# Opening of an adaLN transformer block: unread matmuls out, one term of a sum earlier, the first operand written in halves

## The chip, the cores and the metric

The kernel runs on one core of a Trainium2 chip. The metric is the device time of one execution in microseconds (us); where several executions are given, it is their median. The engines are named as in the profile: PE (TensorE: matmuls), PEld (its weight loads), DVE (VectorE), ACT (ScalarE), POOL (GpSimd), SP (SyncE, which issues most of the DMAs). Each engine runs its own instructions in order; they wait for each other by semaphores.

## The reference, cut to what matters

The reference is one transformer block with adaptive layer norm: a linear attention and a bilinear feed-forward part, on 2048 tokens of width 512. Six modulation vectors come out of one small product with a conditioning vector.

```python
mod = (_silu(c) @ w_mod).reshape(c.shape[0], 6, 1, -1)      # c: (1, 512), w_mod: (512, 3072)
sa, ca, ga, sb, cb, gb = (mod[:, 0], ..., mod[:, 5])
h = _layernorm(x, axis=-1) * (1 + ca) + sa
x = x + ga * _A_ref(h, A_wqkv, A_wo)      # linear attention, 32 heads
h = _layernorm(x, axis=-1) * (1 + cb) + sb
x = x + gb * _B_ref(h, B_w_gate, B_w_up, B_w_down)
```

Only the opening is touched: the layer norm of the first 512 tokens, the vectors `ca` (scale, vector 1) and `sa` (shift, vector 0), the modulated `h`, and the first product of `h` with the key weights.

## The kernel before, in words

Matmuls work in fp32r, and each fp32 product is made of three: a value is split into a high part `h` (rounded to fp32r) and a low part `l` (what is left), and high times high, high times low and low times high are summed in PSUM. The tokens are worked in four chunks of 512 (four groups of 128 tokens, called token groups 0 to 3), the width 512 in four blocks of 128. The order of all work is written out by hand: each engine executes its instructions in the order in which the program text issues them.

The opening does this for chunk 0:

- `keep_on(n)` issues n matmuls of 128x512 on a tile of zeros into a PSUM bank (`ps_idle`) whose result nobody reads (L155). There are 13 at the start, 5 after the small transpose of `c`, and then pairs between the steps of the opening.
- `n0.stats`, `rstd_of`, `nmr_of` and `xhat` are the layer norm: statistics on DVE, 1/std on POOL (L264), the negative mean times 1/std (`nmr`) on DVE (L269), the normalized tile on ACT (L279) or on DVE (L276, token group 3).
- `transpose_token(j)` turns token group j with four PE transposes (L293), one into each of four PSUM banks, so that bank k holds block k of the width for all 512 tokens.
- The columns of `ca` and `sa` for a block of 128 widths come from w_mod in two ways. `block_pe(v, b)` does the whole sum on PE: eight recorded matmuls with one column of output (L402). `half_sum(v, half, *ks)` adds four terms, one for each block of the conditioning vector, for 256 widths at a time: the first term on ACT (L178), the others on DVE (L182); `block_one(v, b)` then sums over the partitions with a matmul against ones (L413, two recorded instructions). `block_out(b)` copies the two columns of block b out of PSUM (L417, DVE).
- `mod_h(k)`, `mod_f(k)` and `mod_l(k)` make the modulated operand of block k: its high part on ACT (L424) from the PSUM bank, the unrounded value on ACT (L431), the low part on DVE (L436). `weight_h(k)` (ACT, L441) and `weight_l(k)` (DVE, L444) split the key weight of block k.
- `cells(*tk, parts)` is the product itself, one 128x512 matmul for token group t, block k and part (L453): part 0 is high times high, part 1 high times the weight's low part, part 2 low times high. The first ones use token groups 0 and 1, parts 0 and 1, then token groups 2 and 3, then part 2 of all four.

The loads are issued by SP and ACT at the start in the order of use; the change leaves them as they are.

Of the kernel before, what the change touches and what calls it, by code (L numbers as in the profile page):

```python
# [9 lines left out]
F32R = mybir.dt.float32r  # L10
AF = mybir.ActivationFunctionType
# [3 lines left out]
P = 128  # L15
# [7 lines left out]
def tile_adaln_block(  # L23
# [12 lines left out]
    nc = tc.nc  # L36
# [4 lines left out]
    NJ = 4  # L41
# [23 lines left out]
    def f32(ap):  # L65
        return ap.bitcast(F32)
# [3 lines left out]
    def T(p, tag, shape=(P, D), dt=F32, bufs=None):  # L70
        cnt[0] += 1
        return p.tile(list(shape), dt, tag="t" if p is tiles else tag, name=f"{tag}_{cnt[0]}", bufs=bufs)

    def B(tag, shape=(P, D), dt=F32):

        return T(tiles, tag, shape, dt)
# [76 lines left out]
    def keep_on(n):  # L153
        for _ in range(n):
            nc.tensor.matmul(ps_idle, idle[:, :P], idle, start=True, stop=True)  # L155
# [18 lines left out]
    def mod_acc(acc, raws, ks, on=None):  # L174
        for k in ks:
            if k == 0:
                if on:
                    on.activation(acc, raws[k], AF.Copy, scale=sc[:, 0:1])  # L178
                else:
                    nc.vector.tensor_scalar(acc, raws[k], sc[:, 0:1], None, op0=ALU.mult)  # L180
            else:
                nc.vector.scalar_tensor_tensor(acc, raws[k], sc[:, k:k + 1], acc, op0=ALU.mult, op1=ALU.add)  # L182
# [201 lines left out]
    n0 = norm[0]  # L384
    both = consts.tile([P, KD, 2], F32, name="both")
    ca, sa = both[:, :, 0], both[:, :, 1]
# [9 lines left out]
    def sums_in(b):  # L396
        return ps_idle if b == 1 else ps_m

    def block_pe(v, b):
        at, ps = at_of(v, b), sums_in(b)  # L400
        for k, raw in enumerate(half_of(v, b)):
            nc.tensor.matmul(ps[:, at:at + 1], raw, sc[:, k:k + 1], start=k == 0, stop=k == KD - 1)  # L402
# [3 lines left out]
    def half_sum(v, half, *ks, on=None):  # L406
        if 0 in ks:
            sums[v, half] = B("f")[:, :D // 2]
        mod_acc(sums[v, half], [raw_half[v, half][k // 2][:, k % 2] for k in range(KD)], ks, on)
# [6 lines left out]
    def block_out(b):  # L416
        nc.vector.tensor_tensor(both[:, b], sums_in(b)[:, 2 * b:2 * b + 2], unit, op=ALU.add)  # L417

    halves = {}

    def mod_h(k):
        halves[k] = (B("h", dt=F32R), B("h", dt=F32R), B("f"))
        h, l, f = halves[k]
        nc.scalar.activation(h, n0.ps[k], AF.Identity, scale=ca[:, k:k + 1], bias=sa[:, k:k + 1])  # L424

    def mod_f(k, on=None):
        h, l, f = halves[k]
        if on:
            on.tensor_scalar(f, n0.ps[k], ca[:, k:k + 1], sa[:, k:k + 1], op0=ALU.mult, op1=ALU.add)
        else:  # L430
            nc.scalar.activation(f, n0.ps[k], AF.Identity, scale=ca[:, k:k + 1], bias=sa[:, k:k + 1])  # L431
        n0.ps[k] = None
# [6 lines left out]
    def weight_h(k):  # L439
        wk.append((B("w", dt=F32R), B("w", dt=F32R)))  # L440
        nc.scalar.activation(wk[k][0], raw_k[k], AF.Copy)  # L441

    def weight_l(k, on=None):
        (on or nc.vector).tensor_tensor(wk[k][1], raw_k[k], f32(wk[k][0]), op=ALU.subtract)  # L444
# [3 lines left out]
    def cells(*tk, parts=(0, 1, 2)):  # L448
        for part in parts:
            for t, k in tk:  # L450
                h, l = halves[k][:2] if k in halves else n0.t[k]
                x, w = ((h, wk[k][0]), (h, wk[k][1]), (l, wk[k][0]))[part]
                nc.tensor.matmul(kps[t], x[:, t * P:(t + 1) * P], w, start=k == 0 and part == 0,  # L453
                                 stop=k == KD - 1 and part == 2)
# [13 lines left out]
    n0.rstd_of(2, 4)  # L468
    n0.transpose_token(0)
    half_sum(0, 0, 0, on=nc.scalar)  # L470
    n0.nmr_of(2, 4)
    n0.xhat(2)
    n0.xhat(3, on=nc.vector)
    keep_on(2)
    n0.transpose_token(1)
    block_pe(1, 0)
    half_sum(0, 0, 1, 2, 3)
    weight_h(0)
    keep_on(2)
    n0.transpose_token(3)  # L480
    n0.transpose_token(2)
    block_one(0, 0)
    block_out(0)
    weight_l(0)
    half_sum(1, 1, 0, on=nc.scalar)
    mod_h(0)
    keep_on(2)
    block_pe(1, 1)
    block_one(0, 1)
    mod_f(0)  # L490
# [10 lines left out]
    cells((2, 0), (3, 0), parts=(0, 1))  # L501
    cells(*four(0), parts=(2,))
    mod_h(1)
    weight_h(1)
    half_sum(0, 1, 1)
# [9 lines left out]
        block_one(1, b)  # L515
        block_one(0, b)
    cells(*four(1), parts=(1, 2))
    weight_l(2)
    block_out(2)
    block_out(3)  # L520
    mod_h(2)
    mod_f(2)
    mod_h(3)
# [1022 lines left out]
```

## Time and profile before

| what | value |
|---|---|
| three executions | 555.76 us median (555.52 to 556.16) |
| the profiled execution | 555.36 us |
| its span, first to last instruction | 553.5 us |
| mean granted TensorE clock | 0.998 |
| busy: PE, DVE, ACT, POOL | 547.2, 419.8, 297.1, 176.9 us |
| first cell (L453) | starts at 14.10 us |

Times of instructions are counted from the start of the span. A row of the timeline has the start, the length, the engine, the line and operation, output and inputs, their shapes, the number of instructions merged in the row, and in brackets the idle time of the engine before it and what ended it. Matmuls overlap: the next one starts before the one ahead has ended, so their cost is read from start to start.

### The profile page before, as it was taken

The numbers are of one execution on the slowest core, as the hardware profiler recorded it, in microseconds if no ns is written. First come the engines' busy times: TensorE is split into PE (matmuls) and PEld (weight loads), VectorE is DVE, ScalarE is ACT, GpSimd is POOL, SyncE is SP. The second block draws the span as 40 slices with busy tenths as digits, with TensorE's granted clock in tenths as the row PEclk, the third lists the DMA queues.
The fourth block names the chain that finished last, engine by engine and source line by source line (L and its number), as shares of the span: only waits on it lengthen the run. The fifth ranks groups of instructions, "written<-read, shape, count | busy, mean of one in ns | idle before, by whom it ended". The sixth has DMA issues, their size and how long they took to land.

```text
span 553.5 us, 8031 instructions
## 1 busy us (share of the span) xinstructions
PE 547.2 (99%) x2741; PEld 459.6 (83%) x2741; DVE 419.8 (76%) x755; ACT 297.1 (54%) x528; POOL 176.9 (32%) x183
## 2 busy tenths in 40 slices
PE   8999999999999999999999999999999999999997
PEld 6888888888888888888888888878888888888886
DVE  6868779978998998865655767854567877879696
ACT  4976858456567876653545355432442534453540
POOL 2000000003527645343556644400512524242400
PEclk9999999999999999999999999999999999999999
DMA  8900224203240045195888635499575534342004
GB/s 286 384 14 1 76 77 152 77 0 78 78 114 2 0 159 183 39 312 183 285 284 273 224 123 205 149 376 325 177 270 192 173 129 149 121 144 86 0 1 152
DMA packets 56752, 83.75 MB, mean 151 GB/s; under 512 B 6596, under 2 KB 21704, under 8 KB 56712
## 3 DMA queue, kind: packets, MB, share of 16 engines
q1 hardware_dynamic: 55872, 82.20, 43.4%
q10 hardware_dynamic: 840, 1.05, 0.5%
q8 instruction: 21, 0.34, 0.2%
q14 instruction: 19, 0.16, 0.1%
HBM read 53.54 MB, written 29.69 MB: 150 GB/s over the span
## 4 chain that ended last, share of the span: by engine, by line
PE 98%; DMA 1%; DVE 0%; ACT 0%; POOL 0%; issue 0%; DVEq 0%; POOLq 0%
PE bank L1037 38%; PE acc L1196 8%; PE acc L851 8%; PE bank L221 5%; PE bank L223 5%; PE bank L222 5%; PE acc L1120 4%; PE acc L1119 4%; PE acc L1121 4%; PE acc L372 3%; PE acc L370 3%; PE acc L371 3%; PE bank L286 2%; PE acc L453 2%; PE bank L826 1%; PE acc L776 1%
## 5 line engine op out<-in xcount | busy, mean ns | idle before, releaser
L1037 PE MATMUL bank<-h,w 128*128 128x512 f32 (+1 forms) x924 | 220.5, 391 | 0.0
L1037 PEld LDWEIGHTS bank<-h,w 128*128 128x128 f32 (+1 forms) x924 | 168.7, 186 | 36.6 <-issue 0.4
L1043 ACT ACTIVATE bank<-bank 128x512 f32<-128x512 f32 (+1 forms) x45 | 26.2, 581 | 131.2 <-PE bank L1037 130.9
L1000 POOL TENSOR_TENSOR w<-raw,w 128x256 fp32r<-128x256 f32 (+3 forms) x22 | 24.3, 1102 | 79.7 <-ACT w L993 64.9
L1220 DVE TENSOR_TENSOR x<-acc,x 128x256 f32<-128x256 f32 x108 | 39.2, 413 | 10.5 <-PE acc L1196 10.0
L1196 PE MATMUL acc<-w,kh 128*128 128x256 f32 x252 | 46.8, 282 | 0.0
L221 PE MATMUL bank<-w,h 128*128 128x512 f32 x112 | 44.1, 394 | 0.0
L1196 PEld LDWEIGHTS acc<-w,kh 128*128 128x128 f32 x252 | 41.4, 191 | 3.1 <-DVE x L1220 0.2
L223 PE MATMUL bank<-w,h 128*128 128x512 f32 x112 | 43.7, 390 | 0.0
L222 PE MATMUL bank<-w,h 128*128 128x512 f32 x112 | 43.7, 390 | 0.0
L851 PE MATMUL acc<-w,xh 128*128 128x512 f32 x128 | 40.7, 399 | 0.0
L1063 DVE TENSOR_TENSOR phi<-bank,g 128x512 f32<-128x512 f32 (+1 forms) x22 | 15.1, 687 | 29.9 <-PE bank L1037 28.4
L700 POOL TENSOR_TENSOR f<-h,zb 128x512 f32<-128x512 f32 x12 | 17.5, 1468 | 62.9 <-ACT zb L680 48.8
L264 POOL TENSOR_TENSOR rstd<-ve,half 128x4 f32<-128x4 f32 (+3 forms) x12 | 10.6, 881 | 82.5 <-DVE ve L261 70.1
L1093 DVE TENSOR_TENSOR g<-bank,u 128x512 f32<-128x512 f32 (+1 forms) x22 | 15.2, 689 | 28.3 <-ACT u L1043 26.9
L1119 PE MATMUL acc<-w,kh 128*128 128x512 f32 (+1 forms) x92 | 35.9, 390 | 0.0
L1120 PE MATMUL acc<-w,kh 128*128 128x512 f32 (+1 forms) x92 | 35.9, 390 | 0.0
L1121 PE MATMUL acc<-w,kl 128*128 128x512 f32 (+1 forms) x92 | 35.8, 389 | 0.0
L1196 PE MATMUL acc<-w,kl 128*128 128x256 f32 x126 | 35.6, 283 | 0.0
L1043 ACT ACTIVATE u<-bank 128x512 f32<-128x512 f32 (+1 forms) x44 | 26.2, 595 | 12.6 <-PE bank L1037 12.4
L1126 DVE TENSOR_TENSOR x<-acc,x 128x512 f32<-128x512 f32 x44 | 28.1, 681 | 6.0 <-PE acc L1121 6.0
L1000 POOL TENSOR_TENSOR w<-t,w 128x512 fp32r<-128x512 f32 (+1 forms) x22 | 29.7, 1348 | 0.0
(198 smaller groups left out, 1180.5 us busy)
## 6 DMA issues: line engine op xcount, KB each, us to landing
right<-w SPq DMA_DIRECT2D x56, 256.0 KB, 3.7
w<-right SPq DMA_DIRECT2D x56, 256.0 KB, 3.7
x<-in_A_x_dram SPq DMA_DIRECT2D x22, 256.0 KB, 5.3
raw<-in_w_mod_dram SPq DMA_DIRECT2D x22, 256.0 KB, 3.5
raw<-in_B_w_down_dram SPq DMA_DIRECT2D x20, 256.0 KB, 3.1
side_s<-h SPq DMA_DIRECT2D x16, 256.0 KB, 2.8
h<-side_s SPq DMA_DIRECT2D x16, 256.0 KB, 5.5
raw<-in_A_wqkv_dram SPq DMA_DIRECT2D x12, 256.0 KB, 5.4
```

The lines of the kernel that those rows point to most:

```text
L221: nc.tensor.matmul(ps, ah, bh, start=begin and i == 0, stop=False)
L222: nc.tensor.matmul(ps, ah, bl, start=False, stop=False)
L223: nc.tensor.matmul(ps, al, bh, start=False, stop=end and i == n - 1)
L851: nc.tensor.matmul(yps[i], x, y, start=fresh and k + n == 0, stop=k == KD - 1 and n == 2, skip_group_check=True)
L1000: sub = lambda out, x, y: (on or nc.gpsimd).tensor_tensor(out, x, f32(y), op=ALU.subtract)
L1037: mm = lambda x, y, **kw: nc.tensor.matmul(ps, x[:, k], y, skip_group_check=True, **kw)
L1043: nc.scalar.activation(out, x, AF.Copy)
L1119: nc.tensor.matmul(dn[j], hh[:n, a:b], dh[:n], start=i == 0, stop=False)
L1120: nc.tensor.matmul(dn[j], hh[:n, a:b], dl[:n], start=False, stop=False)
L1121: nc.tensor.matmul(dn[j], hl[:n, a:b], dh[:n], start=False, stop=i == n_of - 1)
L1196: mm = lambda x, y, **kw: nc.tensor.matmul(ps, x[:, a:b], y, skip_group_check=True, **kw)
L1220: nc.vector.tensor_tensor(xt[:, halves[at]], banks[b][:, part], xt[:, halves[at]], op=ALU.add)
```

## The change

Two of the pairs of unread matmuls go (the one ahead of the transposes of token groups 3 and 2, and the one ahead of `block_pe(1, 1)`); the pairs after token group 0 and the matmuls at the start stay. The second term of the first sum of the shift is issued on DVE ahead of `nmr_of(2, 4)` and no longer behind the normalization of token group 3. The first `mod_h` is written by two ACT instructions, for token groups 0 and 1 and for 2 and 3. `weight_l(2)` is issued behind the two `block_out` calls of blocks 2 and 3. The one-column sum `block_one(0, 0)` stands behind the transposes of all token groups, as before.

```diff
-    def mod_h(k):
-        halves[k] = (B("h", dt=F32R), B("h", dt=F32R), B("f"))
-        h, l, f = halves[k]
-        nc.scalar.activation(h, n0.ps[k], AF.Identity, scale=ca[:, k:k + 1], bias=sa[:, k:k + 1])
+    def mod_h(k, a=0, b=NJ):
+        if not a:
+            halves[k] = (B("h", dt=F32R), B("h", dt=F32R), B("f"))
+        h = halves[k][0][:, a * P:b * P]
+        nc.scalar.activation(h, n0.ps[k][:, a * P:b * P], AF.Identity, scale=ca[:, k:k + 1], bias=sa[:, k:k + 1])
...
     half_sum(0, 0, 0, on=nc.scalar)
+    half_sum(0, 0, 1)
     n0.nmr_of(2, 4)
     n0.xhat(2)
     n0.xhat(3, on=nc.vector)
     keep_on(2)
     n0.transpose_token(1)
     block_pe(1, 0)
-    half_sum(0, 0, 1, 2, 3)
+    half_sum(0, 0, 2, 3)
     weight_h(0)
-    keep_on(2)
     n0.transpose_token(3)
     n0.transpose_token(2)
     block_one(0, 0)
     block_out(0)
     weight_l(0)
     half_sum(1, 1, 0, on=nc.scalar)
-    mod_h(0)
-    keep_on(2)
+    mod_h(0, 0, 2)
+    mod_h(0, 2, 4)
     block_pe(1, 1)
...
     cells(*four(1), parts=(1, 2))
-    weight_l(2)
     block_out(2)
     block_out(3)
+    weight_l(2)
     mod_h(2)
```

Two pairs out are four matmuls; the halves add one ACT instruction. The other instructions are the same on each engine.

## The prediction

> **What bounds the kernel now.** I read the page first (busy shares and the chain of waits), then the windows view over the opening and the rest, then the waits, and last the timeline of the opening, row by row. The page:
>
> ```profile
> PE 547.2 (99%) x2741; PEld 459.6 (83%) x2741; DVE 419.8 (76%) x755; ACT 297.1 (54%) x528; POOL 176.9 (32%) x183
> PE 98%; DMA 1%; DVE 0%; ACT 0%; POOL 0%; issue 0%; DVEq 0%; POOLq 0%
> ```
>
> PE carries the span. The windows view, for all engines in the first row and for PE alone in the second (columns: stretch, its length, busy us and instructions of each engine, granted clock, DMA share, GB/s):
>
> ```profile
> 20.70:549.50 528.80, 528.73 (x2649) 444.61 (x2647) 405.18 (x715) 285.22 (x509) 173.59 (x166) 1.00 0.42 145
> 8.74:12.15 3.41, 3.41 (x28) 1.00 1.09 361
> ```
>
> From 20.70 us to the last matmul PE idles 0.07 us, so whatever the opening wins or loses at 20.70 arrives at the end. In the opening PE is full too, but partly with the unread matmuls. The timeline of the opening, PE first (start, length, engine, line, operation):
>
> ```profile
> 10.78 0.70 PE L155 MATMUL acc<-w 128*128 128x512 f32 x2
> 11.32 1.03 PE L293 MATMUL bank<-ident,n 128*128 128x128 f32 x8
> 12.31 0.35 PE L413 MATMUL acc<-ones,f 128*128 128x1 f32 x2
> 12.52 0.71 PE L155 MATMUL acc<-w 128*128 128x512 f32 x2
> 13.07 0.95 PE L402 MATMUL acc<-sc,raw 128*128 128x1 f32 x8
> 13.88 0.36 PE L413 MATMUL acc<-ones,f 128*128 128x1 f32 x2
> 14.10 1.40 PE L453 MATMUL acc<-w,h 128*128 128x512 f32 x5
> ```
>
> Matmuls overlap, so the cost of a group is the distance from its start to the next group's start: the two pairs (L155) cost 11.32 - 10.78 = 0.54 and 13.07 - 12.52 = 0.55, together 1.09 us. This is the most that removing them can give, beside small waits. Whether PE can use it depends on the chain through DVE and ACT:
>
> ```profile
> 9.12 0.49 ACT L178 ACTIVATE f<-raw,sc 128x256 f32<-128x256 f32 x1
> 9.98 0.16 DVE L269 SCALAR_TENSOR_TENSOR nmr<-mv,rstd 128x2 f32<-128x2 f32 x1 [0.81 <-POOL rstd L264]
> 10.18 0.81 ACT L279 ACTIVATE n<-x,nmr,rstd 128x512 f32<-128x512 f32 x1 [0.56 <-DVE nmr L269]
> 10.18 0.55 DVE L276 TENSOR_SCALAR n<-x,rstd,nmr 128x512 f32<-128x512 f32 x1
> 10.64 1.52 DVE L182 SCALAR_TENSOR_TENSOR f<-raw,sc,f 128x256 f32<-128x256 f32 x3
> 12.70 0.16 DVE L417 TENSOR_TENSOR both<-acc,unit 128x2 f32<-128x2 f32 x1 [0.54 <-PE acc L413]
> 12.78 0.69 DVE L444 TENSOR_TENSOR w<-raw,w 128x512 fp32r<-128x512 f32 x1
> 12.90 0.78 ACT L424 ACTIVATE h<-bank,both 128x512 fp32r<-128x512 f32 x1 [0.98 <-DVE both L417]
> 13.39 0.48 DVE L182 SCALAR_TENSOR_TENSOR f<-raw,sc,f 128x256 f32<-128x256 f32 x1
> 13.58 0.77 ACT L431 ACTIVATE f<-bank,both 128x512 f32<-128x512 f32 x1
> 14.24 0.51 ACT L178 ACTIVATE f<-raw,sc 128x256 f32<-128x256 f32 x1
> 14.36 1.00 DVE L182 SCALAR_TENSOR_TENSOR f<-raw,sc,f 128x256 f32<-128x256 f32 x2
> 14.64 0.78 ACT L424 ACTIVATE h<-bank,both 128x512 fp32r<-128x512 f32 x1
> ```
>
> **The change part by part.** All steps are built in the profiled execution's own time, 555.36 us (span 553.5, 1.9 around it); the median of the three runs is 555.76, 0.4 more, and the difference found is taken off that.
>
> *The second term ahead of nmr.* DVE sits idle for 0.81 us before nmr. ACT's first term ends at 9.61, so the second term can run from 9.65 (0.04 for the hand-over, as from nmr's end at 10.14 to 10.18) to 10.13. An independent DVE operation starts about 0.08 before the one ahead ends (10.64 against 10.73), so nmr starts at 10.05 instead of 9.98: nmr, the waiting ACT normalization and DVE's own lose 0.07. They now run from 10.25 to 11.06 and 10.80. The other two terms take 1.00 (the x2 row at 14.36), from 10.71 to 11.71; before, the sum ended at 12.16. Gain of the sum: 0.45.
>
> *First pair out.* PE is done with its eight L402 at 10.78, but the transposes of token 3 need DVE's normalization: 10.80 + 0.06, so 10.86. Eight transposes took at most 0.99 (11.32 to 12.31), so PE is through them by 11.85. The one-column sum L413 needs the sum plus the 0.15 that the hand-over took before (12.16 to 12.31): 11.86 instead of 12.31. So this pair gives 0.45, not 0.54, because the sum is next late. In the code that sum stands behind all transposes in both kernels; nothing moves there.
>
> *Second pair out.* L402 follows L413 after 0.21 (12.31 to 12.52), takes 0.81, and the second L413 0.22: the cells may start at 11.86 + 0.21 + 0.81 + 0.22 = 13.10 instead of 14.10. Their operand h must be there.
>
> *h in halves.* L417 moves from 12.70 to 12.25, and h from 12.90 to 12.45. No row shows a 128x256 activation out of PSUM. The ends are 0.39 (half of 0.78) and 0.78 (no saving); the nearest rows are the 128x256 ones at 0.49 and 0.51 on the same engine, and I take 0.52. The first half ends at 12.97, and the cells (0.05 later) could start at 13.02: hidden under PE's own 13.10, by a margin of 0.08. Undivided h would have ended at 13.23 and cost 0.18 here. But ACT pays: one activation hands over 0.10 before its end (12.90 to 13.58 for 0.78), so two halves hold it 0.84 and not 0.68. f starts at 12.45 + 0.84 = 13.29, against 13.58: ACT has gained 0.29 where DVE has 0.45. Queued behind it on ACT are the next sum's first term (14.24), h of the second block (14.64) and the second weight (15.30 below).
>
> From here the cells need, in turn, these rows:
>
> ```profile
> 15.28 0.68 DVE L436 TENSOR_TENSOR h<-f,h 128x512 fp32r<-128x512 f32 x1
> 16.02 0.53 PEld L453 LDWEIGHTS acc<-w,h 128*128 128x128 f32 x3 [0.26 <-DVE h L436]
> 15.30 0.63 ACT L441 ACTIVATE w<-raw 128x512 fp32r<-128x512 f32 x1
> 16.28 0.68 DVE L444 TENSOR_TENSOR w<-raw,w 128x512 fp32r<-128x512 f32 x1
> 16.88 1.00 DVE L182 SCALAR_TENSOR_TENSOR f<-raw,sc,f 128x256 f32<-128x256 f32 x2
> 17.95 0.95 PE L413 MATMUL acc<-ones,f 128*128 128x1 f32 x8
> 18.40 0.68 DVE L444 TENSOR_TENSOR w<-raw,w 128x512 fp32r<-128x512 f32 x1
> 19.00 0.22 DVE L417 TENSOR_TENSOR both<-acc,unit 128x2 f32<-128x2 f32 x2
> ```
>
> The low half of h (L436): DVE runs the weight's low part at 12.33, one term at 12.94, L417 of block 1 at 13.34 (its PE input is ready at 13.28), two terms from 13.42 to 14.42, and L436 at 14.34, the spacings as before; f is ready at 14.06. So 14.34 instead of 15.28, gain 0.94, and PE, which reaches that point at 13.10 + 1.92 = 15.02 (14.10 to 16.02 before), starts it at 15.09, 0.07 behind L436's end.
>
> The one-column sums at 17.95: the second of them needs the sum that ends at 17.88, which is queued behind L444 at 16.28, which needs ACT's weight at 15.30. ACT's side gains only 0.29: 15.01 to 15.64, L444 at 15.68, where DVE would be free at 14.34 + 1.00 = 15.34. So L444 gains 0.60, and the sum ends at 17.28. PE comes there at 17.95 - 0.94 = 17.01, spends 0.13 on the two instructions of the first sum and then waits until 17.28 + 0.15 = 17.43 where it had 18.08: **gain 0.65**. That is the new late link: 0.29 of the 0.94 goes into a wait for the ACT chain.
>
> *weight_l(2) behind L417.* Before, DVE held L417 until L444 let it go, at 19.00. PE's sums would end at 18.89 - 0.65 = 18.24 and L417 run at 18.28; with L444 ahead it would run at 17.80 + 0.60 = 18.40. The move gives 0.12 to ACT's next h. PE needs that h only at 20.70 - 0.65 = 20.05, while it ends at about 18.47 + 0.78 = 19.25, and the weight now ends at 19.1 and is needed at 20.5. Both are covered by the cells of block 1, so I count nothing.
>
> Sum: 0.65 us. With halves at 0.39, ACT would not bind and the gain is about 0.94; with halves at 0.78, it falls to about 0.1. My 0.52 gives 0.65, and I expect 0.5 to 0.8. **555.76 - 0.65 = 555.1 us.**
>
> **The rivals.** *The clock falls.* The unread pairs are also the only 512-column work between 9.5 us and the cells. What a cold TensorE costs, and what came before the one fall of the clock in this trace:
>
> ```profile
> 1.98 4.80 PE L155 MATMUL acc<-w 128*128 128x512 f32 x13 [1.98 <-DVE w L150]
> 20.70 2.92 PE L453 MATMUL acc<-w,h 128*128 128x512 f32 x12
> 548.04:551.46 3.42, 1.45 (x13) 1.00 0.67 224
> 551.46:553.47 2.01, 0.00 (x0) 0.00 (x0) 0.00 (x0) 0.00 (x0) 0.00 (x0) 0.50 0.14 47
> ```
>
> The first 13 matmuls took 4.80 us where 12 later took 2.92, 13 thus 3.15: one cold stretch costs 1.65. The clock fell to 0.50 after 3.42 us of which PE had worked 1.45. In the changed kernel PE stays occupied between 9.5 and 13.1 but for some 0.2 us, with transposes and one-column matmuls; before, 8.74 to 12.15 was full in the same loose sense and kept 1.00. Against the rival speaks that occupation; for it, that about 2.0 of those 3.6 us would be one-column matmuls, which move next to nothing. If it decides, one cold stretch over the cells gives 1.65 - 0.65 = 1.0 slower, 556.8; if the clock does not come back at the first chance, two give 2.65 slower, 558.4. It decides where such a stretch with under about 1.45 us of wide work counts as idle. The Trainium skill, "TensorE: Matmul & The Clock Gate", Part 1 (the HAM clock gate), says that the gate judges free-running windows of about 3.4 us, and Part 4 (PE-mode transpose) that a transpose doesn't count as busy in the same way. By that rule the pairs would be what kept the clock, and the time would be that of this rival in those runs whose window falls into the gap; the fall at the end of this trace agrees with a window of that length, and no row here shows a transpose stretch without pairs.
>
> *ACT's halves cost next to nothing and PE takes all.* The two pairs and the waits around them give 1.2 together: 554.5, faster than the bound. Against it speaks the ACT chain above.
>
> *Nothing arrives.* If halves cost as much as whole activations, 0.1 remains: 555.7. The same comes out if a load that doesn't move binds first. These rows say it doesn't:
>
> ```profile
> 9.13 1.85 SPq L111 DMA_DIRECT2D raw<-in_A_wqkv_dram  x3
> DMA to landing us min/median/max: 5.1/5.1/5.1
> 13.56 5.07 SPq L111 DMA_DIRECT2D raw<-in_A_wqkv_dram  x8
> ```
>
> The load behind L441's weight is issued at 9.13 and lands 5.1 later, at 14.2, for a use at 15.0. No issue moves past another in the queues.
>
> **How the numbers follow.** What a measurement of this kernel can tell from no change is about 0.2%, 1.1 us. My forecast has 0.64, nothing arrives 0.08, all taken 0.07, one cold stretch 0.09, more than one or another loss of that size 0.12. Faster by over 0.2% is the third alone, 0.07; slower the last, 0.12; the rest, 0.81, lies within. The forecast's own range is 554.8 to 555.5; the range given reaches from all taken to one cold stretch, 554.5 to 556.8.
>
> **What would show it.** Right: no L155 row after 9.7 us; cells (now L454) starting near 13.1; the second one-column sum near 17.4 with a PE wait of about 0.3 before it; 20.70 moved to about 20.05; halves of h near 0.52. Wrong: cells spaced 0.42 and not 0.23 apart, or a clock under 1.00 before 20 us (the first rival); halves above 0.6 with the second weight after 15.3 (nothing arrives); a new PE wait after 20 us.

## The result, and the profile after

The changed kernel takes 556.38 us (median of 22 executions, 555.52 to 559.48), the kernel before in the same sessions 555.98 (22, 555.27 to 556.66): a ratio of 1.0019, with a 95% interval of 1.0010 to 1.0028. The medians are 0.4 us apart; the ratio follows the means, 556.88 and 555.84, which are 1.0 apart. By either it is slower, where 0.65 us less was forecast. (One execution of a later experiment, e11, 682.98 us at a mean clock of 0.754, is of another, slow state and is left out.)

The executions of the changed kernel are not of one kind. Twelve have a mean granted clock of 0.998 or more; they take 555.52 to 556.41, and their middle, 555.94, is that of the kernel before. The other ten have 0.992 to 0.995 and take 556.90 to 559.48. The kernel before has none of the second kind in 108 executions. So two things are to be explained: why ten executions lose clock, and why the twelve that keep it gain nothing.

The profiled execution of the changed kernel is one that lost clock: 556.9 us, span 554.9. From its page, the busy shares and the granted clock in 40 slices:

```profile
PE 548.2 (99%) x2737; PEld 460.6 (83%) x2737; DVE 419.8 (76%) x755; ACT 297.2 (54%) x529; POOL 177.8 (32%) x183
PEclk9899999999999999999999999999999999999999
```

Four matmuls fewer, one activation more, as the diff says. The second slice, 13.9 to 27.7 us, shows an 8. The windows view (stretch, its length, busy us and instructions of PE, PEld, DVE, ACT and POOL, granted clock, DMA share, GB/s) around it:

```profile
10.20:13.62 3.42, 3.42 (x30) 3.22 (x30) 2.81 (x9) 2.69 (x6) 0.02 (x1) 1.00 1.09 359
13.62:17.03 3.41, 3.41 (x9) 2.66 (x9) 3.08 (x8) 3.41 (x8) 0.00 (x0) 0.50 1.06 388
17.03:20.44 3.41, 3.41 (x20) 2.94 (x20) 1.82 (x6) 1.65 (x4) 0.00 (x0) 1.00 1.05 386
```

The clock was halved for one stretch of 3.41 us. In the 3.42 us ahead of it PE is busy without a gap. The timeline of the changed kernel shows with what:

```profile
10.13 0.95 PE L402 MATMUL acc<-sc,raw 128*128 128x1 f32 x8
11.05 1.09 PE L293 MATMUL bank<-ident,n 128*128 128x128 f32 x8
12.07 0.35 PE L413 MATMUL acc<-ones,f 128*128 128x1 f32 x2
12.29 1.03 PE L402 MATMUL acc<-sc,raw 128*128 128x1 f32 x8
12.66 1.02 ACT L425 ACTIVATE h<-bank,both 128x256 fp32r<-128x256 f32 x2 [0.48 <-DVE both L417]
13.41 2.31 PE L454 MATMUL acc<-w,h 128*128 128x512 f32 x5
18.74 0.95 PE L413 MATMUL acc<-ones,f 128*128 128x1 f32 x8
26.95 0.39 PE L221 MATMUL bank<-w,h 128*128 128x512 f32 x1
```

One-column matmuls, transposes, and 0.21 us of the cells: no L155 row. The cells begin at 13.41, 0.69 earlier than before, but five of them now take 2.31 where they took 1.40. The second one-column sum starts at 18.74 (17.95 before), and the first matmul of the query projection (L221), with which the opening is over, stands at 26.95. Before:

```profile
26.18 0.39 PE L221 MATMUL bank<-w,h 128*128 128x512 f32 x1
549.22 0.28 PE L1492 MATMUL bank<-w,kl 96*128 96x256 f32 x1
549.99 0.81 SPq L1222 DMA_DIRECT2D out_dram<-x  x2
```

The changed kernel comes to L221 0.77 late, of which 0.23 is a later start of its transposes (8.80 and 8.57), and keeps that distance to the last matmul. The span, however, is longer by 1.4. The rest is behind the last matmul; the end of the changed kernel:

```profile
550.00 0.28 PE L1493 MATMUL bank<-w,kl 96*128 96x256 f32 x1
550.77 1.08 SPq L1223 DMA_DIRECT2D out_dram<-x  x2
```

Before, the last matmul ends at 549.50 and the span at 553.5: a tail of 3.98 us (from the unrounded end). After, it is 4.61: SP's last two issues take 1.08 and not 0.81, and then the last transfer lands later. The view of that one transfer gives 2.0 us from issue to landing before (first row) and 2.3 after (second row):

```profile
DMA to landing us min/median/max: 2.0/2.0/2.0
DMA to landing us min/median/max: 2.3/2.3/2.3
```

### The profile page after: what moved, and what is told of

Same layout as the page of the kernel before. It is cut to its first block, busy times and chain, and to the rows that moved or that the text cites. A ratio compares the mean times of both kernels' runs of the same rounds, so it can differ in the third digit from the quotient of the medians.

```text
span 554.9 us, 8027 instructions
## 1 busy us (share of the span) xinstructions
PE 548.2 (99%) x2737; PEld 460.6 (83%) x2737; DVE 419.8 (76%) x755; ACT 297.2 (54%) x529; POOL 177.8 (32%) x183
## 4 chain that ended last, share of the span: by engine, by line
PE 99%; DVE 0%; issue 0%; DVEq 0%
PE bank L1038 38%; PE acc L1197 8%; PE acc L852 8%; PE bank L221 5%; PE bank L223 5%; PE bank L222 5%; PE acc L1120 4%; PE acc L1121 4%; PE acc L1122 4%; PE acc L372 3%; PE acc L370 3%; PE acc L371 3%; PE acc L454 2%; PE bank L286 2%; PE acc L155 1%; PE bank L827 1%
## 5 line engine op out<-in xcount | busy, mean ns | idle before, releaser
L221 PE MATMUL bank<-w,h 128*128 128x512 f32 x112 | 44.1, 394 | 0.0
```

What stands on the lines that cost most here:

```text
L221: nc.tensor.matmul(ps, ah, bh, start=begin and i == 0, stop=False)
```

## The experiments

Every kernel was run in the same sessions as the kernel before, which took 555.46 beside the first four kernels (27 executions), 555.70 beside the next four (33) and 555.77 beside the last three (26). "Executions that lost clock" are those with a mean granted clock of at most 0.996. "Tail" is the time from the end of the last matmul to the end of the span, "opening" the time from the first transpose to the first L221, both in the profiled execution. The opening is counted from the first transpose because its start moves from execution to execution: in the profiles here the transposes start between 8.55 and 9.18.

| kernel | median us | ratio, 95% interval | lost clock | opening | tail |
|---|---|---|---|---|---|
| before | 555.98 | 1 | 0 of 108 | 17.61 | 3.98 |
| after | 556.38 | 1.0019, 1.0010 to 1.0028 | 10 of 22 | 18.15 | 4.61 |
| e1_pairs_back | 556.23 | 1.0012, 1.0003 to 1.0021 | 0 of 11 | 17.36 | 4.97 |
| e2_pairs_out_alone | 557.88 | 1.0046, 1.0033 to 1.0058 | 5 of 5 | 18.78 | 4.65 |
| e3_wide_columns | 555.71 | 1.0005, 0.9996 to 1.0014 | 0 of 11 | 16.92 | 4.63 |
| e4_all_pairs_out | 556.76 | 1.0019, 1.0009 to 1.0029 | 6 of 11 | 18.12 | 4.62 |
| e5_wide_weight_first | 555.38 | 0.9994, 0.9985 to 1.0003 | 0 of 11 | 17.42 | 3.98 |
| e6_weight_later_alone | 556.37 | 1.0013, 1.0004 to 1.0021 | 0 of 11 | 17.65 | 4.80 |
| e7_one_pair_back | 556.19 | 1.0009, 1.0000 to 1.0018 | 0 of 11 | 17.13 | 4.66 |
| e8_last_store_on_act | 555.07 | 0.9990, 0.9981 to 0.9999 | 0 of 11 | 17.12 | 3.88 |
| e9_shorter_start | 554.93 | 0.9986, 0.9978 to 0.9995 | 0 of 11 | 17.14 | 3.88 |
| e10_store_alone | 555.73 | 0.9999, 0.9991 to 1.0008 | 0 of 11 | 17.66 | 4.21 |
| e11_change_store | 557.42 | 1.0027, 1.0010 to 1.0044 | 5 of 8 | 18.38 | 4.71 |

The ratio follows the means, so where executions of both kinds occur it says more than the medians. Opening and tail are those of one execution of each kernel.

### Do the pairs keep the clock?

**e1_pairs_back**: the change with both pairs put back.

```diff
+    keep_on(2)
     n0.transpose_token(3)
...
     mod_h(0, 2, 4)
+    keep_on(2)
     block_pe(1, 1)
```

> The changed kernel with both pairs of unread matmuls put back; the early second term, the halves of h and the later weight_l(2) stay. Theory clock (the pairs kept the TensorE clock up, and without them it falls to half for 3.4 us in some executions): no execution with a mean clock under 0.997, the cells 0.23 us apart, the first L221 (start of the q projection) near 26.1 us against 26.18 before, time within 0.3 us of before. Theory order (the moved term, the halves or the moved weight cost the time): as slow as the changed kernel or slower, some 556.4 to 557.4 us, with PE waiting in the opening.

No execution lost clock, as the theory of the clock had it, and yet it is 0.8 us slower than the kernel before by the medians (556.23 and 555.46), which neither theory explains: the clock theory had it within 0.3, and the other put the loss into the opening. Its opening is 0.25 shorter than before's, its tail 0.99 longer: the first sign that the end of the kernel matters, and that it was not the clock alone.

**e2_pairs_out_alone**: the kernel before without the two pairs, and nothing else.

```diff
-    keep_on(2)
     n0.transpose_token(3)
...
     mod_h(0)
-    keep_on(2)
     block_pe(1, 1)
```

> The kernel before with the two pairs out and nothing else changed. Theory clock: about half of the executions with a mean clock of 0.995 or less (as 10 of 22 of the changed kernel had), each about 1.5 us longer than the rest; in an execution without it the first L221 starts near 25.8 us. Theory order: no fall of the clock beyond what the kernel before shows, and a time of 0.3 to 0.5 us under before.

All five executions lost clock. The windows view and two rows of the timeline of this kernel:

```profile
9.90:14.52 4.62, 4.19 (x35) 3.79 (x34) 3.21 (x9) 2.81 (x6) 0.70 (x1) 1.00 1.09 366
14.52:17.93 3.41, 3.41 (x9) 2.65 (x10) 3.29 (x9) 3.41 (x7) 0.00 (x0) 0.50 1.06 387
```

```profile
12.99 0.35 PE L413 MATMUL acc<-ones,f 128*128 128x1 f32 x2 [0.43 <-DVE f L182]
14.40 1.99 PE L453 MATMUL acc<-w,h 128*128 128x512 f32 x4
```

Without the earlier second term PE waits 0.43 for the sum, the stretch without wide work lasts until 14.40, and the fall comes every time, again for 3.41 us. Taking the pairs out is enough to lose the clock. Whether the rest of the change, which shortens the stretch, makes the fall rarer (5 of 5 here, 10 of 22 there), so few executions don't show.

**e3_wide_columns**: the change, with the recorded one-column matmuls of `block_pe` widened to 64 equal columns, of which one is read. No pair is put back.

```diff
-            nc.tensor.matmul(ps[:, at:at + 1], raw, sc[:, k:k + 1], ...)
+            nc.tensor.matmul(ps[:, at:at + 64], raw, sc[:, k:k + 1].to_broadcast([P, 64]), ...)
```

> The changed kernel, but the one-column sums of block_pe write 64 equal columns each (the same scalar column broadcast; 63 are not read). Theory clock, with a gate that goes by the columns that stream through the array: the 16 matmuls at L402 still start 0.11 us apart, no execution falls to a mean clock of 0.995, and with the clock kept the first L221 starts near 25.5 us, time some 0.65 us under before. If the gate goes by wide matmuls or by something else: cold executions as often as in the changed kernel. Theory order: as the changed kernel, without regard to the clock.

No execution lost clock, nor did one in e5, e8 and e9 below, which keep the wide columns (0 of 44 in all). No other line of the changed kernel was touched: with the pairs out, the clock fell because these matmuls were narrow. The timeline of this kernel, the same stretch:

```profile
10.98 1.09 PE L293 MATMUL bank<-ident,n 128*128 128x128 f32 x8
12.20 1.08 PE L402 MATMUL acc<-sc,raw 128*128 128x64 f32 x8
12.57 1.02 ACT L425 ACTIVATE h<-bank,both 128x256 fp32r<-128x256 f32 x2 [0.46 <-DVE both L417]
13.32 1.38 PE L454 MATMUL acc<-w,h 128*128 128x512 f32 x5
14.50 0.69 DVE L437 TENSOR_TENSOR h<-f,h 128x512 fp32r<-128x512 f32 x1
15.21 0.64 ACT L442 ACTIVATE w<-raw 128x512 fp32r<-128x512 f32 x1
15.88 0.69 DVE L445 TENSOR_TENSOR w<-raw,w 128x512 fp32r<-128x512 f32 x1 [0.30 <-ACT w L442]
17.55 0.74 PEld L413 LDWEIGHTS acc<-ones,f 128*128 128x128 f32 x6 [0.15 <-DVE f L182]
25.62 0.39 PE L221 MATMUL bank<-w,h 128*128 128x512 f32 x1
```

Eight matmuls of 64 columns take 1.08 where eight of one column took 1.03 in the changed kernel (12.29): the 64-fold work is nearly free. The eight weight loads beside them (PEld) are busy for 0.97 us in both kernels, so it is probably these that set the pace. The five cells are back at 1.38, and L221 stands at 25.62, 0.56 earlier than before although the transposes start 0.13 later. So the opening does win 0.69 when the clock stays. But the time is no better than before, where 0.65 us less was expected: the tail is 4.63.

**e4_all_pairs_out**: the change without the remaining pair (issued behind token group 3's normalization in the program text; on PE it stands behind the transposes of token group 0).

```diff
     n0.xhat(3, on=nc.vector)
-    keep_on(2)
```

> The changed kernel with the last pair (behind the transposes of token group 0) out too, so that no unread matmul is left between 8.3 us and the cells. Theory clock: cold executions are more frequent than 10 of 22 and last for one stretch or two, median 557 to 558 us. Theory order: a little faster than the changed kernel, by up to 0.3 us, since PE loses half a microsecond of work ahead of a wait.

Six of 11 lost clock, about as many as in the changed kernel. That the fall would come more often with a still longer stretch is not borne out: 6 of 11 against 10 of 22 can't be told apart. The ratio is the same 1.0019.

**e7_one_pair_back**: the change with the second pair alone put back, ahead of `block_pe(1, 1)`.

```diff
     mod_h(0, 2, 4)
+    keep_on(2)
     block_pe(1, 1)
```

> The changed kernel with one of the two pairs back, the one ahead of block_pe(1, 1); SyncE's program has 605 instructions. Theory clock: with 0.55 us of wide matmuls in the middle of the gap the clock falls seldom or never (less than 10 of 22), the cells start near 13.6 us, the end is 4.6 us after the last matmul, so the time is near 556.0 us. Should a single pair not count, the clock falls as often as in the changed kernel.

One pair in the middle of the stretch is enough: none of 11 lost clock. (By the medians it is still 0.5 us slower than the kernel before; its tail is a long one, 4.66.) It costs 0.2 of the opening's gain against e3 (17.13 and 16.92; nmr stands 1.49 behind the first transposes in both). The timeline of this kernel:

```profile
12.66 0.70 PE L155 MATMUL acc<-w 128*128 128x512 f32 x2
```

### What is lost at the end?

**e6_weight_later_alone**: the kernel before with the one line that the prediction counted at nothing.

```diff
-    weight_l(2)
     block_out(2)
     block_out(3)
+    weight_l(2)
```

> The kernel before with weight_l(2) behind the two block_out calls and nothing else changed; SyncE's program has 605 instructions and not 604. Theory count: the opening as before (first L221 near 26.2 us in an execution whose clock rises early), but 4.6 us instead of 4.0 from the last matmul to the end, and some 0.6 us slower. Theory opening: no difference, or 0.1 us faster.

It costs 0.67 us by the medians (556.37 and 555.70; ratio 1.0013, 1.0004 to 1.0021), and not in the opening (17.65 against 17.61). The last rows of this kernel's timeline and, from its views of transfers, the last transfer and the queue of instruction fetches in 1.1 us around its landing (packets, MB, share of 16 engines' time):

```profile
549.88 0.28 PE L1492 MATMUL bank<-w,kl 96*128 96x256 f32 x1
550.65 1.08 SPq L1222 DMA_DIRECT2D out_dram<-x  x2
```

```profile
DMA to landing us min/median/max: 2.5/2.5/2.5
q14 instruction: 1, 0.01, 5.6%
```

**e5_wide_weight_first**: e3 with `weight_l(2)` back in its old place.

```diff
+    weight_l(2)
     block_out(2)
     block_out(3)
-    weight_l(2)
```

> The wide one-column sums of e3_wide_columns, but weight_l(2) stands ahead of the two block_out calls again, as before the change. SyncE's program has 604 instructions then, as in the kernel before; it has 605 or 606 in all slower kernels so far. Theory count (SyncE stalls 0.3 us at a fixed place of its program; with 602 profiled instructions that falls on a wait, with 603 or 604 on the issue of the last output transfer): no stall ahead of the last issue, 4.0 us from the last matmul to the end and not 4.6, first L221 near 25.6 us, time some 0.5 us under before. Theory opening (the end of the kernel has nothing to do with it): as e3_wide_columns, no faster than before.

The tail is before's again, to the hundredth, and the time is the first below it, though the interval of the ratio still reaches 1.0003. Its end:

```profile
549.40 0.28 PE L1493 MATMUL bank<-w,kl 96*128 96x256 f32 x1
550.17 0.81 SPq L1223 DMA_DIRECT2D out_dram<-x  x2
```

```profile
DMA to landing us min/median/max: 2.0/2.0/2.0
q14 instruction: 1, 0.01, 1.7%
```

The two ends differ in three things: the last two issues take 0.81 or 1.08, the last transfer lands after 2.0 or 2.5, and near its landing the fetch of 8 KB of instructions takes 1.7% or 5.6% of 16 x 1.1 us, 0.30 or 0.99 us. What the line changes for SP is the waits (counted among SP's records in the traces): SP executes 602 instructions in the kernel before and in e5, 603 in e6 and 604 in the changed kernel. The ones added are waits early in its stream, each ahead of a load of w_mod: one ahead of the load issued at 92 us (e6 and the changed kernel), one ahead of that issued at 74 us (the changed kernel). For what they wait was not followed up. The issues themselves are the same and in the same order.

The move is not the only way to get there. e2, which leaves `weight_l(2)` where it was, has 603 instructions on SP and a tail of 4.65. So leaving out the pairs alone brings the long tail too. In all kernels whose output is issued wholly by SP, 602 instructions go with a tail of 3.98 (before, e5), and 603 or 604 with 4.61 to 4.97 (the other seven). The packet records show where the fetch falls: before and in e5 it starts 2.57 and 2.58 us behind the last matmul, when the last packet of the output has ended (2.34 and 2.33); in the changed kernel and e6 it starts at 1.81 and 1.91, and the output ends only at 3.11 and 3.30. It is so in all kernels here: the fetch starts behind the last output packet in the five with a tail of 3.88 to 4.21, and ahead of its end in the eight with 4.61 to 4.97. That one wait more decides where the fetch falls fits the kernels whose output SP issues; how it does so, and whether the fetch delays the output or both follow from something else, no run shows. The Trainium skill, "Runtime: NRT & Kernel Launch", section "Instruction fetch mechanics", has the cost of going on to the next block of instructions as mostly hidden. These rows agree for the body of the kernel, where PE in the kernel before idles 0.07 us in all from 20.70 to the last matmul, and differ at its end, where an early and long fetch goes with a late landing.

The forecast of 25.6 for L221 was missed: it stands at 26.35, of which 0.23 is a later start (transposes at 8.93 and 8.70 in e3). The other 0.5 is in the opening, and the timeline of this kernel shows where it begins:

```profile
9.84 0.51 ACT L178 ACTIVATE f<-raw,sc 128x256 f32<-128x256 f32 x1 [0.26 <-DMA raw<-in_w_mod_dram]
10.38 0.48 DVE L182 SCALAR_TENSOR_TENSOR f<-raw,sc,f 128x256 f32<-128x256 f32 x1 [0.70 <-ACT f L178]
10.78 0.15 DVE L269 SCALAR_TENSOR_TENSOR nmr<-mv,rstd 128x2 f32<-128x2 f32 x1
```

In this execution the first term waited for its load, the second term, now ahead of nmr on DVE, waited for the first, and nmr stands 1.85 behind the first transposes where e3 has 1.49 (10.19) and before 1.41. The moved term has tied the normalization to a load that it did not depend on. In e6, which has the old order, the first term waits for the same load, and nmr still stands 1.45 behind the first transposes (10.63 and 9.18):

```profile
9.79 0.51 ACT L178 ACTIVATE f<-raw,sc 128x256 f32<-128x256 f32 x1 [0.19 <-DMA raw<-in_w_mod_dram]
10.63 0.16 DVE L269 SCALAR_TENSOR_TENSOR nmr<-mv,rstd 128x2 f32<-128x2 f32 x1 [0.81 <-POOL rstd L264]
```

**e8_last_store_on_act**: e3 with the very last output transfer issued by ACT.

```diff
-                    nc.sync.dma_start(ov[ch, j][:, halves[at]], ...)
+                    (nc.scalar if (ch, j, at) == (3, 3, 0) else nc.sync).dma_start(ov[ch, j][:, halves[at]], ...)
```

> e3_wide_columns with the last output transfer issued by ScalarE instead of SyncE. Theory count: the stall of SyncE no longer stands ahead of that transfer, so the end comes 4.0 us or less after the last matmul and the time is 0.5 us or more under before. Theory opening: as e3_wide_columns.

Its tail is 3.88, and it is faster than the kernel before: 555.07, ratio 0.9990 (0.9981 to 0.9999). (In its profile nmr also stands late, 1.72 behind, after a wait of 0.20 for the same load; its opening is 0.2 longer than e3's.) Its end:

```profile
549.72 0.33 SPq L1223 DMA_DIRECT2D out_dram<-x  x1
550.06 0.37 ACTq L1223 DMA_DIRECT2D out_dram<-x  x1
```

**e10_store_alone** and **e11_change_store**: the same line in the kernel before and in the change as it stands.

> The kernel before with the last output transfer on ScalarE and nothing else changed. Theory count: SyncE's stall didn't stand ahead of that transfer in the kernel before, so the end stays 3.9 to 4.0 us behind the last matmul and the time within 0.2 us of before. If instead ScalarE's queue is faster as such, the time falls by 0.3 us or more.

> The changed kernel with the last output transfer on ScalarE, so that the stall at the end is gone and the fall of the clock is left. Theory clock: about half of the executions at a mean clock of 0.995 or less, near 556.5 us; the others near 555.1 us, as e8_last_store_on_act.

In the kernel before it brings nothing (0.9999): the short tail was there already. In its profile the tail is even 4.21, where 3.9 to 4.0 was expected; the output ends as early as in e8, 2.24 behind the last matmul, and why the span ends 0.33 later is open. In the change it doesn't help: the executions that kept their clock take 555.68 to 556.12, where less was expected. ACT's issue comes as early as in e8, counted from the last matmul, but the transfer lands late and the fetch is long:

```profile
551.19 0.37 ACTq L1223 DMA_DIRECT2D out_dram<-x  x1
```

```profile
DMA to landing us min/median/max: 2.8/2.8/2.8
q14 instruction: 1, 0.01, 5.4%
```

So the slow issue on SP alone is not the cause of the long tail. What goes with it in both e6 and e11 is the early and long fetch; e11's SP stream has one wait more than e8's (255 against 254). In e8 it was therefore probably the number of waits, and not the engine that issues, that shortened the end; the runs don't separate the two. A count of all instructions is no rule here: e11's SP executes 602, as the kernel before's does, and has the long tail.

**e9_shorter_start**: e8 with 11 unread matmuls at the start and not 13.

```diff
-    keep_on(13)
+    keep_on(11)
```

> e8_last_store_on_act (wide one-column sums, last output transfer on ScalarE) with 11 and not 13 unread matmuls at the start. Theory phase (in executions whose clock rises late, near 7.5 us, the slow first 13 hold up the small transpose of c and with it the normalization): 0.2 to 0.3 us less in the median than e8's 555.07, the first transposes never later than 8.9 us. If two matmuls fewer let the clock rise later or fall: cells 0.43 us apart, 1 us or more slower.

554.93 us, ratio 0.9986 (0.9978 to 0.9995): the fastest of all, and like e8 faster than both kernels. Whether the shorter start adds to e8 is open: 0.14 less by the medians where 0.2 to 0.3 was expected, the two intervals overlap, and both openings are 17.1.

## Why the prediction was wrong, point by point

**The opening's sum was right, for a PE at full clock and an early first term.** The comparison is with e3, where the clock stays, counted from the first transposes (8.57 before, 8.70 in e3).

- "Second term ahead of nmr": nmr was to lose 0.07. It starts 1.41 behind the transposes before (9.98 - 8.57), 1.45 after (10.25 - 8.80) and 1.49 in e3: it loses 0.04 to 0.08. But this holds only where the first term is early, as it was in the profile of before; in e5 nmr loses 0.44, and with it the opening gains 0.19 and not 0.69. That nmr now waits for ACT's first term and its load was not named as a new wait.
- "First pair out": the transposes of token group 3 were to start 2.29 behind (10.86 - 8.57); they start 2.28 behind (10.98).
- "Second pair out": the cells were put 4.53 behind (13.10) and come 4.62 behind (13.32). The eight L402 take 0.89 to the next group in the changed kernel (12.29 to 13.18), 0.92 with 64 columns in e3 (12.20 to 13.12), and not 0.81.
- "h in halves": 0.52 each was taken between 0.39 and 0.78; the pair took 1.02, and f on ACT starts 0.91 behind the first half (12.66 to 13.57), with 0.84 predicted. ACT did become the late link: L445 waits 0.30 for L442.
- The low half of h: 5.77 behind predicted (14.34), 5.80 measured (14.50).
- The second one-column sum: predicted at 17.43, 8.86 behind; its load starts at 17.55, 8.85 behind. The wait in front of it is 0.15 and not 0.3: PE came to the sums 0.06 later than predicted (17.20 in e3, 8.50 behind, for 17.01, 8.44 behind) and took longer over the first. The gain of 0.65 at this place was met, and L221 gains 0.69.

**Two steps failed.** The first is the weight given to "The clock falls". Against that rival stood "that occupation", and that the stretch from 8.74 to 12.15 "was full in the same loose sense and kept 1.00". But that stretch held two pairs, and 10.20 to 13.62 in the changed kernel holds none; a busy PE was the wrong measure. The bar of about 1.45 us of wide work was too high as well: in e7 one pair, 0.54 us from its start to the next group's, kept the clock. The rival's price of 1.65 for a cold stretch was too high: the openings of the changed kernel and e3 differ by 1.23 (18.15 and 16.92), those of e11 and e8, where nmr stands 1.72 behind in both, by 1.26 (18.38 and 17.12). The chance was 0.21 for all falls together, as if one case would hold for every execution; the runs show a fall in 10 of 22. The prediction names runs "whose window falls into the gap", but none of its cases has executions of both kinds in one median.

The Trainium skill's rule that was cited, from "TensorE: Matmul & The Clock Gate", Part 1, windows of about 3.4 us, agrees with each fall in the four profiles that have one: 3.41 or 3.42 us long. That they come in some executions only agrees with windows that run free of the kernel's start. The clock records show such a grid: before, the clock rises at 5.33 and falls at 551.46, 160 times 3.413 us later; in the changed kernel it rises at 6.79, falls at 13.62, rises at 17.03 and falls at 552.92, which is 2, 1 and 157 such steps. The same page's advice in "HAM oscillation — how this bites in real kernels", no idle gaps of PE over about 3.4 us, was kept here and wasn't enough: PE has no gap in 10.20 to 13.62, and the clock fell. The rule of Part 4 that a transpose doesn't count in the same way is not contradicted, but it is not the whole of it: e3 has the same transposes, and 64 columns for one in L402 keep the clock.

The second step is "whatever the opening wins or loses at 20.70 arrives at the end". It arrives at the last matmul: L221 and the last matmul are late by the same 0.77 and 0.78 in the changed kernel. At the end of the span it arrives with another loss on top, because the 3.98 us behind the last matmul were taken as fixed and no row of them was read. "weight_l(2) behind L417" was counted at nothing by looking at DVE, ACT and PE; it costs 0.67 (e6), and its trace is in SP's stream, which issues nothing new. "No issue moves past another in the queues" was true, and not enough: waits were added between them.

**The balance.** For the executions that kept the clock: the opening gives -0.69 at best (e3; -0.2 to -0.5 where the first term is late, by e5, e8 and e9), the tail +0.63 (4.61 - 3.98), together about 0; the medians are 555.94 and 555.98. The ones that lost it pay for a cold stretch, 1.2 to 1.3 us by the openings; the seven with a clock of 0.994 to 0.995, 556.9 to 558.0 us, lie 1.0 to 2.1 above the 555.94. The other three, with 0.992 to 0.993, took 558.6 to 559.5 us, 2.7 to 3.5 above. None of them was profiled, but their mean clock allows an estimate: in the profiled execution 3.41 us in the opening and 1.97 at the end at half clock go with 0.995, and 0.992 to 0.993 means 7.8 to 8.9 us at half clock, about what two such stretches and the end would make. With 10 of 22 that lost clock the median comes out 0.4 above the kernel before, and the mean 1.0. The two losses come apart: e1, e3 and e7 take the first away and keep the second, and e6 has only the second.

## What to carry to other kernels

Before unread or seemingly idle matmuls are taken out, list what PE does in each 3.4 us around them by width and not by busy time: here a stretch of one-column matmuls and transposes lost the clock while PE showed 100%. The remedy was nearly free here: 64 equal columns for one in matmuls that each load a new 128x128 weight. And when a change is worth less than 1 us, read the tail behind the last matmul too, and run each "free" line of the diff by itself: here the one counted at nothing cost as much (0.67) as the rest can gain (0.69).

## What the runs showed of the hardware that was not expected

- The clock fell to 0.50 for 3.41 us behind a stretch in which PE was busy throughout; by their mean clocks 10 of 22 executions had such a fall. With two 128x512 matmuls in the middle of the stretch (0 of 11), or 64 columns for one in 16 matmuls (0 of 44 in e3, e5, e8 and e9), it did not come.
- A matmul of 64 columns in fp32 costs next to what one of a single column does: eight in 1.08 and 1.03 us.
- A wait more in SP's stream, at 74 or 92 us, goes with a tail that is 0.6 to 1.0 us longer at the end (in kernels whose output SP issues). An 8 KB instruction fetch then starts ahead of the end of the last output transfer and takes 0.6 to 1.0 us; where the tail is 3.88 to 4.21 it starts behind it and takes 0.3 to 0.5.
